# The feed-forward of the last two units of a two-layer attention and MLP kernel, done jointly by Strassen's scheme

## The chip, the cores and the metric

The kernel runs on one core of one Trainium2 chip. A core has five engines with queues of their own: TensorE (PE in the profile; its weight loads are PEld), VectorE (DVE), ScalarE (ACT), GpSimd (POOL) and SyncE (SP), which here only issues transfers. The metric is the device time of one execution in microseconds. The kernel before takes 1161.14 us, the median of three runs (1160.39 to 1161.52).

## The reference

The input x is one sequence of 2048 tokens by 640. Two layers with the same weights run one after the other, each an attention over 8 earlier tokens at distance 2 (32 heads of 20) and then an MLP.

```python
def _A_ref(x, wqkv, wo):
    ...
    logits = jnp.einsum("bhsd,bhswd->bhsw", q, kg) * scale
    logits = jnp.where(mask[None, None, :, :], logits, -1e9)
    attn = _softmax(logits, axis=-1)
    o = jnp.einsum("bhsw,bhswd->bhsd", attn, vg)
    return (lambda x, *d: x.transpose(*d))(o, 0, 2, 1, 3).reshape(B, S, D) @ wo

def _B_ref(x, w1, b1, w2, b2):
    y = _layernorm(x, axis=-1)
    h = _gelu(jnp.einsum("bsd,df->bsf", y, w1) + b1)
    return jnp.einsum("bsf,fd->bsd", h, w2) + b2

x = A_x
x = x + _A_ref(_layernorm(x, axis=-1), A_wqkv, A_wo)
x = x + _B_ref(_layernorm(x, axis=-1), B_w1, B_b1, B_w2, B_b2)
x = x + _A_ref(_layernorm(x, axis=-1), A_wqkv, A_wo)
x = x + _B_ref(_layernorm(x, axis=-1), B_w1, B_b1, B_w2, B_b2)
```

D is 640 and F is 1536.

## The kernel before

The tokens are cut into four groups of 512 (4 row tiles of 128). A group in one layer is a unit; `N` is 8 units, 0 to 7, and units 6 and 7 are the last two groups of the second layer. A unit passes through `layernorm`, `qkv`, `attention` (mostly DVE, in four groups of heads), `project` (the `wo` matmul, L766, and its residual on DVE, L772), a second `layernorm` and `mlp`.

Every matrix product is done in three passes of fp16: both operands are split into a high and a low half, and `PASS` names the pairs (high by high, high by low, low by high). So one step over 128 of K is three matmuls. The weights are scaled by `WS` = 64, split once at the start and kept in DRAM (`mw[0]` for W1, `mw[1]` for W2, twelve blocks of 128 of F each), from where every unit loads them again through the tiles c1 and c2 (names c_78 to c_83 in the order's rows).

`mlp` runs over the twelve F blocks. For each it does 5 K steps of W1 by the transposed activations yT (15 matmuls of 512 columns into a bank ps, L824), the gelu on ACT (L830), the high half on ACT (L833), the low half on DVE (L835), and then for four row tiles the product with W2 (24 matmuls, 512 and 128 columns wide alternately, into five accumulator banks, L846). At the end DVE adds the accumulators to x (L882) and SP stores the rows.

yT comes from DMA transposes that SP issues (L578 after `layernorm`, L755 for the input of `project`). In the last layer the bias b2 is added to x ahead of time, on POOL (L584) or, for unit 7, on DVE (L587).

Nothing runs in the order in which it is written. Each piece of work is given to `Plan` with its engine, a duration, a priority, what it needs and gives, and which buffers it uses; `Plan.run` plays the engines forward with these numbers and writes the instructions out in the order that comes of it. On the chip each engine runs its own queue in that order and waits on semaphores. Operations whose kind stands in `PAIRS` are marked: `Plan` lets long POOL instructions of that kind start only where DVE's marked ones do not run.

## Time and profile before

| what | value |
| --- | --- |
| median of three runs | 1161.14 us |
| span of the profiled execution | 1158.8 us |
| around the span (median less span) | 2.3 us |
| first matmul of all MLPs, L824, share of the chain | 26.6% |
| second matmul, L846, share of the chain | 26.6% |
| qkv, L610, share of the chain | 33.5% |
| `project`, L766, share of the chain | 11.3% |
| last attention instruction on DVE, end | 973.1 us |
| last matmul, end | 1155.17 us |

The profile is one execution recorded by the hardware profiler. The chain of waits starts from the last instruction and goes back, at each step, to what released it; an engine that holds nearly all of the chain sets the time. Rows of groups read: line, engine, operation, tiles out and in, shapes, count, then busy time in us and the mean length of one in ns, then the idle time of the engine before them. Rows of the timeline read: start in us, length in us, engine, line. The end of a matmul is modelled, so lengths of matmul groups are taken from the chain, where one group ends when the next begins.

### The profile page before, as it was taken

The page shows a single profiled execution, that of the slowest core. Times are in us where ns is not written, and L with a number is a line of the kernel's source. Part 1 is how long each engine was busy: PE and PEld are TensorE (multiplying, and loading weights), DVE is VectorE, ACT ScalarE, POOL GpSimd, SP SyncE. Part 2 cuts the span into 40 slices and gives each one's busy share as a digit, 9 for nine tenths or more (in the row PEclk, how much of TensorE's full clock was granted, in tenths as well). Part 3 has the DMA queues.
Part 4 walks back from the last instruction along what each step waited for, and adds up shares of the span by engine and source line. Part 5 has one row for each costly group of instructions (what it writes and reads, how often), then busy time and mean ns, then how long its engine had stood idle before and what let it go on. Part 6 is the DMA issues. An engine that isn't in the chain of part 4 may idle for free.

```text
span 1158.8 us, 17441 instructions
## 1 busy us (share of the span) xinstructions
PE 1153.2 (100%) x6948; PEld 628.1 (54%) x6948; DVE 980.3 (85%) x935; ACT 512.8 (44%) x931; POOL 113.1 (10%) x96
## 2 busy tenths in 40 slices
PE   9999999999999999999999999999999999999998
PEld 6444446577654565546555555555456555555554
DVE  7899999999999999999999999999999995311212
ACT  6395345445464344823537352376235333521211
POOL 1010002011111111210112011101111010000000
PEclk9999999999999999999999999999999999999999
DMA  9999899988686468665746765577555845533432
GB/s 303 311 297 277 292 343 274 280 285 256 190 267 177 165 176 225 194 178 165 231 163 189 194 193 187 175 188 192 189 186 154 265 142 137 140 103 100 147 102 80
DMA packets 219773, 235.01 MB, mean 203 GB/s; under 512 B 129884, under 2 KB 170412, under 8 KB 219692
## 3 DMA queue, kind: packets, MB, share of 16 engines
q1 hardware_dynamic: 219692, 233.90, 67.7%
q8 instruction: 54, 0.88, 0.3%
q14 instruction: 27, 0.22, 0.1%
HBM read 158.93 MB, written 44.78 MB: 176 GB/s over the span
## 4 chain that ended last, share of the span: by engine, by line
PE 98%; DMA 1%; DVE 0%; issue 0%; SPq 0%; ACT 0%; ACTq 0%
PE ps L610 33%; PE acc L846 27%; PE ps L824 27%; PE ps L766 11%; DMA c<-mw 1%; DMA xf<-in_A_x_dram 0%; PE ps L846 0%; DVE wq L433 0%; DVE bn L522 0%; DVE yT L496 0%; DVE w L564 0%; ACT yT L494 0%; DVE xf L882 0%; SPq L445 0%; SPq L428 0%
## 5 line engine op out<-in xcount | busy, mean ns | idle before, releaser
L610 PE MATMUL ps<-wq,yT 128*128 128x480 f16 (+1 forms) x1950 | 391.0, 363 | 0.3
L846 PE MATMUL acc<-c,act 128*128 128x512 f16 (+1 forms) x2298 | 328.6, 299 | 0.3 <-DMA c<-mw 0.3
L824 PE MATMUL ps<-yT,c 128*128 128x512 f16 (+1 forms) x1620 | 328.1, 355 | 0.0
L610 PEld LDWEIGHTS <-yT 128*128 128x128 f16 x1950 | 189.3, 98 | 198.8 <-issue 0.3
L846 PEld LDWEIGHTS <-act 128*128 128x128 f16 x2310 | 181.7, 98 | 142.3 <-issue 0.5
L824 PEld LDWEIGHTS <-c 128*128 128x128 f16 x1620 | 154.6, 98 | 146.3
L830 ACT ACTIVATE act<-ps,b 128x512 f32<-128x512 f32 (+1 forms) x108 | 68.9, 638 | 286.4 <-PE ps L824 285.9
L694 DVE TENSOR_TENSOR pr<-qk 128x2560 f32<-128x2560 f32 x64 | 180.4, 2820 | 3.5 <-DMA qk<-spill 3.5
L720 DVE TENSOR_TENSOR pr<-sm,v 128x2560 f32<-128x2560 f32 x64 | 179.3, 2817 | 0.3
L698 DVE TENSOR_REDUCE sm<-pr 128x128 f32<-128x2560 f32 x64 | 179.5, 2805 | 0.1
L835 DVE TENSOR_TENSOR act<-act 128x512 f16<-128x512 f32 (+1 forms) x108 | 67.5, 626 | 126.2 <-ACT act L833 125.8
L627 ACT ACTIVATE ev<-ps 128x480 f32<-128x480 f32 x128 | 72.6, 569 | 180.3 <-PE ps L610 169.7
L728 DVE TENSOR_TENSOR pr<-pr 128x1280 f32<-128x1280 f32 (+1 forms) x128 | 144.4, 1148 | 0.1
L766 PE MATMUL ps<-wo,yT 128*128 128x320 f16 x960 | 131.7, 299 | 0.0
L766 PEld LDWEIGHTS <-yT 128*128 128x128 f16 x960 | 93.9, 98 | 37.6
L532 ACT ACTIVATE junk<-xf 128x640 f16<-128x640 f32 x57 | 41.9, 734 | 76.2 <-DVE xf L772 63.1
L742 POOL TENSOR_TENSOR ohl<-w,ohl 128x640 f16<-128x640 f32 x24 | 34.3, 1428 | 340.4 <-DVE pr L694 209.7
L549 POOL TENSOR_TENSOR ln<-ln,half 128x2 f32<-128x2 f32 (+1 forms) x31 | 32.8, 1061 | 337.1 <-ACT ln L546 336.9
L833 ACT ACTIVATE act<-act 128x512 f16<-128x512 f32 (+1 forms) x108 | 62.6, 580 | 2.7
L584 POOL TENSOR_TENSOR xf<-xf,b 128x640 f32<-128x640 f32 x26 | 41.1, 1580 | 185.7 <-DVE act L835 67.6
L576 DVE TENSOR_TENSOR w<-w,w 128x640 f16<-128x640 f32 x60 | 47.9, 816 | 6.3 <-ACT w L574 6.3
L568 ACT ACTIVATE w<-xf,ln 128x640 f32<-128x640 f32 x57 | 50.6, 909 | 3.1 <-DVE w L576 3.1
(57 smaller groups left out, 510.2 us busy)
## 6 DMA issues: line engine op xcount, KB each, us to landing
c<-mw SPq DMA_DIRECT2D x216, 320.0 KB, 3.3
spill<-ev SPq DMA_DIRECT2D x64, 480.0 KB, 4.0
qk<-spill SPq DMA_DIRECT2D x32, 880.0 KB, 5.6
v<-spill SPq DMA_DIRECT2D x32, 880.0 KB, 5.3
qk<-spill SPq DMA_DIRECT2D x32, 320.0 KB, 3.5
act<-in_B_w_dram SPq DMA_DIRECT2D x24, 320.0 KB, 5.3
mw<-c SPq DMA_DIRECT2D x24, 320.0 KB, 5.2
xf<-in_A_x_dram SPq DMA_DIRECT2D x16, 320.0 KB, 6.7
```

The costliest lines, as they stand in the source:

```text
L610: nc.tensor.matmul(ps, transposed(yk)[:, a * KD + k, t * P:(t + 1) * P], wq[:, b, k, g, i0:i1], start=first and j == 0, stop=last and j == ...
L627: act(3 * GC, -400 + n, lambda i=i, pk=pk, ek=ek: nc.scalar.activation(tile_of(*ek)[:, :, i], tile_of(*pk)[:, :3 * GC].rearrange("p (a c) ...
L694: nc.vector.tensor_mul(tile_of(*pk), w[:, HALO + m + t0:HALO + m + t0 + EH, None, :].to_broadcast([P, EH, W, GC]), windows(w, t0, [GC, W], ...
L698: dve(E, G - 0.7, lambda pk=pk, t0=t0: nc.vector.tensor_reduce(lg(t0, t0 + EH).rearrange("p t w h -> p (t w h)"), tile_of(*pk).rearrange(" ...
L720: nc.vector.tensor_mul(tile_of(*vk).rearrange("p t w (h d) -> p t (w h) d", d=DH), lg(t0, t0 + EH).rearrange("p t w h -> p t (w h)")[:, :, ...
L728: dve(EH * w * GC, G - 0.9, lambda vk=vk, w=w: nc.vector.tensor_add(tile_of(*vk)[:, :, 0:w], tile_of(*vk)[:, :, 0:w], tile_of(*vk)[:, :, w ...
L766: nc.tensor.matmul(tile_of(*pk)[:, :D // 2], transposed(yk)[:, a * KD + k, t * P:(t + 1) * P], wo[:, b, k, c * D // 2:(c + 1) * D // 2], s ...
L824: nc.tensor.matmul(tile_of(*pk)[:, :nt], tile_of(*ck)[:, a, k * P:(k + 1) * P], transposed(yk)[:, c * KD + k, t0 * P:t1 * P], start=i == 0 ...
L830: act(nt, -430, lambda pk=pk, h32=h32, e=e: nc.scalar.activation(tile_of(*h32)[:, :nt], tile_of(*pk)[:, :nt], AF.Gelu_apprx_tanh, bias=b1[ ...
L833: act(nt, -440, lambda h32=h32, hk=hk: nc.scalar.activation(tile_of(*hk)[:, 0, :nt], tile_of(*h32)[:, :nt], AF.Copy), need=[("h", j)], giv ...
L835: dve(nt, -1000, lambda h32=h32, hk=hk: nc.vector.tensor_sub(tile_of(*hk)[:, 1, :nt], tile_of(*h32)[:, :nt], tile_of(*hk)[:, 0, :nt]), nee ...
L846: nc.tensor.matmul(to, tile_of(*hk)[:, a, (i - t0) * P:(i - t0 + 1) * P], tile_of(*wk)[:, c, w0:w0 + n], start=first, stop=e == NF - 1 and ...
```

## The change

Units 6 and 7 leave `mlp` and are computed together by a new function `pair`. Their 1024 tokens are two blocks of rows (unit 6, unit 7), F is two halves of six blocks, and D is cut into two halves. With blocks A11, A12 (unit 6) and A21, A22 (unit 7), and B11 to B22 of the weights, Winograd's form of Strassen's scheme needs seven products and sums of blocks before and after them.

In the first matmul K is 640, five blocks of 128: the scheme takes blocks 0, 1 and 2, 3 as the two halves of K, and block 4 is added plainly. `joint` makes the operands for this: unit 7's layernorm on ACT, unit 6's once more on DVE, four sums of 256 columns and one of 128 on DVE, a high and a low half of 1536 columns on ACT and DVE, and two transposes per row tile (twelve blocks of 128 each) into zT, which lies over wq. `sums_of_weights` loads the raw weights again, makes four sums for each block pair (W1 on DVE, 256 wide; W2 on POOL, 320 wide), splits them, stores them in `mt` in DRAM and lets the matmuls load them from there.

For each of the six F blocks `pair` first does P1 (A11 by B11), keeps a copy in A21, goes on in the same bank to C11, and does P1 of the second matmul with it. Then, for each block, P6, P5, P7, P4 and P3 in two banks, with DVE adds between (u2, u3, C22, C21, C12), three gelus, the halves, and P2 of the second matmul; then DVE makes S1 and S2 and POOL makes S3 and S4 of the second matmul's rows. At the end the last five products of the second matmul follow each other, 320 columns wide. All matmuls of `second` are 320 wide. Buffers of the attention (wq, wo, v, ev, qk, pr, ohl) and the rows of x of units 0 and 1, once they are stored, hold the new blocks; the lists in `free` say what must be over before.

The bias b2 of both units is added on POOL. The split end of the last unit (`ENDS`, `cuts`, `fresh`) is gone.

```diff
-ENDS = 2
-PARTS = [(0, 0, 2), (0, 2, 4)] + [(b, 0, 4) for b in range(1, 2 * NU)]
+PARTS = [(0, 0, 2), (0, 2, 4)] + [(b, 0, 4) for b in range(1, 2 * NU - 2)]
+PAIR = (2 * NU - 2, 2 * NU - 1)
+KH = 2
+HALF = D // 2
+NP = NF // 2
...
+    T["raw"] = [pr_flat[0][:, :2 * D], pr_flat[0][:, 2 * D:], pr_flat[1][:, :2 * D]]
+    T["thl"] = [pr_flat[1][:, 2 * D:].bitcast(HT), ohl_flat[:, 2 * D:].bitcast(HT)]
...
+    blocks_of = {"A21": cut(v_flat) + [t[:, :BANK] for t in ev_flat], "A11": cut(wo_flat)}
+    for i, q in enumerate(("A12", "S1", "A22", "HL")):
+        blocks_of[q] = spare[i * NP:(i + 1) * NP]
+    last_n, last_u = PAIR[1], PAIR[1] % NU
...
+        "wq": [("qkvp", last_n, t, g) for t in range(M) for g in range(NG)],
+        "pr": [("o", 2 * NU * NG - 1, a) for a in range(M // EH)] + [("done", 0, i) for i in range(M)],
+        "wo": [("wop", last_n, t, c) for t in range(M) for c in range(2)],
+        "ohl": [("oT", last_n, t) for t in range(M)],
+        "blocks": [("hhi", len(PARTS) * NF - 1), ("hlo", len(PARTS) * NF - 1)] + [("done", u, i) for u in range(2) for i in range(M)] + [("zT", t, a) for t in range(M) for a in range(2)],
...
+        for t in range(M):
...
+            act(D, prio, lambda t=t, both=both: ln(both(0, D), u1, t, col), need=[("r", name1, t), *free["wq"], *free["pr"]],
+                give=[("y", name1, t)], use=[lk, zk], ptr=2)
+            dve(D * 3 // 4, prio, lambda t=t, wk=wk: nc.vector.tensor_scalar(
+                tile_of(*wk), x[u0][:, t], col0(2)[:, t:t + 1], col0(3)[:, t:t + 1], op0=OP.mult, op1=OP.add),
+                need=[("r", name0, t), ("r", name1, t)], give=[("again", t)], use=[lk0, wk, zk])
+            for n, u, ready in ((n0, u0, ("again", t)), (n1, u1, ("y", name1, t))):
+                pool(1.6, -100, lambda t=t, u=u: nc.gpsimd.tensor_add(x[u][:, t], x[u][:, t], b2), need=[ready, "b2"], give=[("xb", n, t)])
+            def sums(both=both, wk=wk):
+                Q = KH * P
+                y = tile_of(*wk)
+                a21, a22, s1, s2, s3, s4 = (both(c, c + Q) for c in (0, Q, D, D + Q, D + 2 * Q, D + 3 * Q))
+                nc.vector.tensor_add(s1, a21, a22)
+                nc.vector.tensor_sub(s3, y[:, :Q], a21)
+                nc.vector.tensor_sub(s2, s1, y[:, :Q])
+                nc.vector.tensor_sub(both(D + 4 * Q, D + 4 * Q + P), y[:, 2 * Q:], both(2 * Q, D))
+                nc.vector.tensor_sub(s4, y[:, Q:2 * Q], s2)
...
+            dve(4 * KH * P + P, prio, sums, need=[("y", name1, t), ("again", t)], give=[("zs", t)], use=[zk, wk], more=0.3)
+            act(ZC, prio, lambda zh=zh, both=both: nc.scalar.activation(tile_of(*zh)[:, 0], both(KH * P, KH * P + ZC), AF.Copy),
+                need=[("zs", t)], give=[("zhi", t)], use=[zk, zh])
+            dve(ZC, prio, lambda zh=zh, both=both: nc.vector.tensor_sub(tile_of(*zh)[:, 1], both(KH * P, KH * P + ZC), tile_of(*zh)[:, 0]),
+                need=[("zhi", t)], give=[("zlo", t)], use=[zk, zh])
+            for a in range(2):
+                dma_transpose(prio, lambda t=t, zh=zh, a=a: nc.sync.dma_start_transpose(
+                    zT[:, a * ZK:(a + 1) * ZK, t * P:(t + 1) * P], tile_of(*zh)[:, a]),
+                    need=[("zlo" if a else "zhi", t)], give=[("zT", t, a)], use=[zh])
...
+    def sums_of_weights(i, e, prio):
...
+        def combine():
+            b11, b12, b21, b22 = (part(0), part(n), part(D), part(D + n)) if i else (part(0), part(D), part(n), part(D + n))
+            by = nc.gpsimd if i else nc.vector
+            for to, a, b in ((b11, b12, b11), (b12, b22, b12), (b22, b22, b11), (b21, b21, b22)):
+                by.tensor_sub(to, a, b)
...
+        if i:
+            pool(3.8, prio, combine, need=needs, give=[("tf", i, e)], use=[rk])
+        else:
+            dve(4 * n, prio, combine, need=needs, give=[("tf", i, e)], use=[rk], more=0.3)
+        act(4 * n, prio, lambda: nc.scalar.activation(halves(0), whole(), AF.Copy, scale=WS), need=[("tf", i, e), *free["ohl"]],
+            give=[("thi", i, e)], use=[rk, sk])
+        dve(4 * n, prio, lambda: nc.vector.scalar_tensor_tensor(halves(1), whole(), WS, halves(0), op0=OP.mult, op1=OP.subtract),
+            need=[("thi", i, e)], give=[("tlo", i, e)], use=[rk, sk])
+        dma(P * 16 * n / 1e3, -300 + prio, lambda: nc.sync.dma_start(
+            mt[i][e].rearrange("p a n -> p (a n)"), tile_of(*sk)[:, :8 * n]), need=[("tlo", i, e)], give=[("mt", i, e)], use=[sk], packet=16 * n)
...
+    def pair():
...
+        def second(to, hl, what, e, tiles, passes, start, prio, need, give, use):
...
+            def product():
+                for i in tiles:
+                    for a, c in passes:
+                        nc.tensor.matmul(tile_of(*to(i))[:, :HALF], hl()[:, a, i * P:(i + 1) * P], half_rows(wk, e)[:, c],
+                                         start=start and (a, c) == PASS[0], stop=(a, c) == PASS[-1], skip_group_check=True)
...
+        def split_block(src, dst, tag, prio, need, use=()):
+            act(BANK, prio, lambda: nc.scalar.activation(dst()[:, 0], src(), AF.Copy), need=need, give=[("hi", tag)], use=use)
+            dve(BANK, prio, lambda: nc.vector.tensor_sub(dst()[:, 1], src(), dst()[:, 0]), need=[("hi", tag)], give=[("lo2", tag)], use=use)
...
+        for e in R:
...
+            wt = partial(tile_of, *ck)
+            after = [("wop", n1, M - 1, 1)] if e < 3 else []
+            first(pk, wt, [(k * P, yb(k)) for k in range(KH)], True, j - 1.0 - AHEAD, [*ready, ck, *after] + [("hi", ("P1", e - 2))] * (e > 1),
+                  [("P1", e)], [yk, ck])
+            act(BANK, -435, lambda pk=pk, e=e: nc.scalar.activation(A21[e], tile_of(*pk), AF.Copy), need=[("P1", e), *free["pr"]],
+                give=[("s1", e)], use=[pk])
+            first(pk, wt, [(k * P, yb(k)) for k in range(KH, KD)], False, j - 1.1 - AHEAD, [("s1", e)], [("C11", e)], [yk, ck])
+            gelu(A11[e], partial(tile_of, *pk), e, ("h11", e), [("C11", e), *free["wo"]], [pk])
+            split_block(lambda e=e: A11[e], partial(tile_of, *hk), ("P1", e), -440, [("h11", e)], [hk])
+            for q, passes in enumerate((PASS[:2], PASS[2:])):
+                second(X, partial(tile_of, *hk), "P1", e, range(M), passes, e == 0, j + 0.05 * q,
+                       [("lo2" if q else "hi", ("P1", e)), *([("XP1", e - 1 + q, q ^ 1)] if e + q else [])], [("XP1", e, q)], [hk])
...
+            T = [[(q * KH * P + k * P, zb(z + k)) for k in range(KH)] for q, z in ((0, 3), (3, 5), (2, 7), (1, 0), (4, 9))]
+            B52, B51 = 10 * P, 11 * P
+            pr = j - 1.0 - AHEAD
+            first(bk, wt, T[1], True, pr, [*zready, *got], [("P6", e)], [dk])
+            first(ck, wt, T[0] + [(B52, zb(2))], True, pr + 0.01, [*zready, *got], [("P5", e)], [dk])
+            dve(BANK, -1001, lambda e=e, bk=bk: nc.vector.tensor_add(A12[e], tile_of(*bk), A21[e]), need=[("P6", e), ("s1", e), *free["blocks"]],
+                give=[("u2", e)], use=[bk])
+            first(bk, wt, T[2], False, pr + 0.02, [("u2", e)], [("P7", e)], [dk])
+            dve(BANK, -1001, lambda e=e, bk=bk: nc.vector.tensor_add(A22[e], tile_of(*bk), A21[e]), need=[("P7", e), *free["blocks"]],
+                give=[("u3", e)], use=[bk])
+            dve(BANK, -1000, lambda e=e, ck=ck: nc.vector.tensor_add(A22[e], tile_of(*ck), A22[e]), need=[("P5", e), ("u3", e)],
+                give=[("C22", e)], use=[ck])
+            first(bk, wt, T[3] + [(B51, zb(2))], False, pr + 0.03, [("u3", e)], [("P4", e)], [dk])
+            first(ck, wt, T[4] + [(B52, zb(11))], False, pr + 0.04, [("C22", e)], [("P3", e)], [dk])
+            dve(BANK, -999, lambda e=e, bk=bk: nc.vector.tensor_add(A21[e], tile_of(*bk), A21[e]), need=[("P4", e)],
+                give=[("C21", e)], use=[bk])
+            dve(BANK, -999, lambda e=e, ck=ck: nc.vector.tensor_add(A12[e], tile_of(*ck), A12[e]), need=[("P3", e)],
+                give=[("C12", e)], use=[ck])
+            gelu(A22[e], lambda e=e: A22[e], e + NP, ("h22", e), [("C22", e)])
+            gelu(A21[e], lambda e=e: A21[e], e, ("h21", e), [("C21", e)])
+            gelu(A12[e], lambda e=e: A12[e], e + NP, ("h12", e), [("C12", e)])
+            split_block(lambda e=e: A12[e], partial(tile_of, *hk), ("P2", e), -445, [("h12", e)], [hk])
+            split_block(lambda e=e: A22[e], lambda e=e: hl_of(HL[e]), ("A22", e), 10 + e, [("h22", e)])
+            dve(BANK, 20 + e, lambda e=e: nc.vector.tensor_add(S1[e], A21[e], A22[e]), need=[("h21", e), ("h22", e)], give=[("S1", e)])
+            dve(BANK, 20 + e, lambda e=e: nc.vector.tensor_sub(A22[e], S1[e], A11[e]), need=[("S1", e), ("lo2", ("A22", e))], give=[("S2", e)])
+            pool(1.2, 20 + e, lambda e=e: nc.gpsimd.tensor_sub(A21[e], A11[e], A21[e]), need=[("S1", e)], give=[("S3", e)])
+            pool(1.2, 20 + e, lambda e=e: nc.gpsimd.tensor_sub(A12[e], A12[e], A22[e]), need=[("S2", e), ("lo2", ("P2", e))], give=[("S4", e)])
+            for q, passes in enumerate((PASS[:2], PASS[2:])):
+                second(X, partial(tile_of, *hk), "P2", e, range(M), passes, False, j + 0.05 * q,
+                       [("lo2" if q else "hi", ("P2", e)), *[("s1x", i) for i in range(M)],
+                        *([("XP2", e - 1 + q, q ^ 1)] if e + q else [])], [("XP2", e, q)], [hk])
...
+        plan_of = (("S2", A22, A11, Y, True), ("S1", S1, A22, X2, True), ("S3", A21, S1, Y, False), ("S4", A12, A21, X2, False), ("A22", None, HL, Y, False))
...
```

DVE's queue around the end of the last `project`, before (acc are the accumulators of unit 5, act the halves of h, w the tiles of the layernorm):

```order
L772 SCALAR_TENSOR_TENSOR xf<-ps_94,xf 128x320
L576 TENSOR_TENSOR w_86<-w_88,w_86 128x640
L772 SCALAR_TENSOR_TENSOR xf<-ps_96,xf 128x320
L576 TENSOR_TENSOR w_84<-w_87,w_84 128x640
L576 TENSOR_TENSOR w_87<-w_85,w_87 128x640
L882 SCALAR_TENSOR_TENSOR xf<-acc_101,xf 128x4x128
L835 TENSOR_TENSOR act<-act 128x512
```

The same place now (the first row is the last residual; wq 128x256 and qk_67 are the z tiles, pr the raw weights):

```order
L808 SCALAR_TENSOR_TENSOR xf<-ps_94,xf 128x320
L933 TENSOR_TENSOR qk_67<-qk_67 128x256
L934 TENSOR_TENSOR qk_67<-w_86,qk_67 128x256
L935 TENSOR_TENSOR qk_67<-qk_67,w_86 128x256
L936 TENSOR_TENSOR qk_67<-w_86,qk_67 128x128
L937 TENSOR_TENSOR qk_67<-w_86,qk_67 128x256
L942 TENSOR_TENSOR wq<-wq 128x1536
L973 TENSOR_TENSOR pr_77<-pr_77 128x256 x4
L973 TENSOR_TENSOR pr_76<-pr_76 128x256 x4
L903 SCALAR_TENSOR_TENSOR xf<-acc_99,xf 128x512
L903 SCALAR_TENSOR_TENSOR xf<-acc_100,xf 128x512
L1036 TENSOR_TENSOR act<-wo,act 128x512 x2
```

Sums of the z operands and of the weights now stand between the last residual and the low halves of h (L1036) for which the second matmul waits.

DVE's queue later, in the MLP of unit 7, before:

```order
L882 SCALAR_TENSOR_TENSOR xf<-acc_100,xf 128x512
L835 TENSOR_TENSOR act<-act 128x512
L587 TENSOR_TENSOR xf<-xf,b_105 128x640
L835 TENSOR_TENSOR act<-act 128x512 x2
L587 TENSOR_TENSOR xf<-xf,b_105 128x640
```

DVE's queue now for the fifth block of the six products (L1131 is u2, L1134 u3, L1136 C22, L1140 C21, L1142 C12, L1149 and L1150 S1 and S2, L988 the low halves of W2 sums, L1036 low halves):

```order
L1131 TENSOR_TENSOR xf<-ps_96,ev_70 128x512
L1036 TENSOR_TENSOR act<-xf,act 128x512
L1150 TENSOR_TENSOR wq<-xf,wo 128x512
L988 SCALAR_TENSOR_TENSOR ohl_75<-pr_76,ohl_75 128x1280
L1134 TENSOR_TENSOR qk_67<-ps_96,ev_70 128x512
L1136 TENSOR_TENSOR qk_67<-acc_101,qk_67 128x512
L1036 TENSOR_TENSOR wo<-qk_67,wo 128x512
L988 SCALAR_TENSOR_TENSOR pr_77<-pr_76,pr_77 128x1280
L1140 TENSOR_TENSOR ev_70<-ps_96,ev_70 128x512
L1036 TENSOR_TENSOR act<-qk_67,act 128x512
L1142 TENSOR_TENSOR xf<-acc_101,xf 128x512
```

Where one instruction per block of F stood, ten or eleven now stand, and the adds u2, u3 and C22, which PE waits for before P7, P4 and P3, come in line with the rest.

SP's queue at the start of the stage, before (ohl is the input of `project`):

```order
L817 DMA c_83<-mw_134 128x1280
L755 DMA_TRANSPOSE yT_73<-ohl_75 128x10x128 x4
L817 DMA c_81<-mw_123 128x1280
L817 DMA c_80<-mw_113 128x1280
```

And now:

```order
L840 DMA c_83<-mw_134 128x1280
L960 DMA pr_76<-in_B_w_dram 128x5x128 x4
L791 DMA_TRANSPOSE yT_73<-ohl_75 128x10x128 x4
L1013 DMA c_81<-mw_123 128x2x320
```

Four loads of raw W1 blocks are issued ahead of the transposes of `project`'s input.

And SP's queue now where the loads of the second block of the six products (yT_73) stand; before, this place held loads of c only:

```order
L1121 DMA yT_73<-mt_136 128x2x1024
L1013 DMA c_82<-mw_131 128x2x320
L1013 DMA c_82<-mw_132 128x2x320
L990 DMA mt_139<-pr_77 128x2048
L1013 DMA c_83<-mw_133 128x2x320
L1013 DMA c_83<-mw_134 128x2x320
L1121 DMA yT_73<-mw_118 128x2x384
L1121 DMA yT_73<-mw_112 128x2x128
```

The last two pieces of the second block now follow the store of the fifth block's weight sums (mt_139).

More of the change, by code (lines that the diff above doesn't have):

```diff
@@ L884, in mlp @@
+        for i in tiles:
+            mm(2 * BANK, 2, j, lambda i=i: outer(i, PASS[:2], [own(i)]),
+               need=[("hhi", j), wk, *before], give=[("outh", b, e, i)], use=[wk, hk, bank(i)])
+            mm(BANK, 1, j - 0.1, lambda i=i: outer(i, PASS[2:], [own(i)]),
+               need=[("hlo", j), ("outh", b, e, i)], give=[("out", b, e, i)], use=[wk, hk, bank(i)])
         dve(REST * (t1 - t0), -991, lambda: add(
```

281 lines of the change are left out of this document (220 added, 61 removed).

## The prediction

> **What bounds the kernel now.** I read the page first: busy shares, the slices, the chain of waits.
>
> ```profile
> PE 1153.2 (100%) x6948; PEld 628.1 (54%) x6948; DVE 980.3 (85%) x935; ACT 512.8 (44%) x931; POOL 113.1 (10%) x96
> PE   9999999999999999999999999999999999999998
> DVE  7899999999999999999999999999999995311212
> PEclk9999999999999999999999999999999999999999
> PE 98%; DMA 1%; DVE 0%; issue 0%; SPq 0%; ACT 0%; ACTq 0%
> ```
>
> PE is busy from end to end at full granted clock, and the chain runs through it for 98% of the span. DVE is full for 33 slices and nearly free in the last seven. Busy time alone would not prove a bound, so next come PE's own waits, in total.
>
> ```profile
> PE acc L906 <- POOL ident L404: 1.4, 1, 1.4
> PE acc L846 <- DMA c<-mw: 0.3, 1, 0.3
> ```
>
> In 1158.8 us PE waited twice, for 1.7 us. A matmul less is time less, and any wait added on PE is time more. Then the chain in order of time, for the stretch the change touches (start, length, what).
>
> ```profile
> 973.12 3.26 PE acc L846 x24
> 976.38 3.24 PE ps L824 x15
> 979.62 16.30 PE ps L766 x120
> 995.92 3.26 PE acc L846 x24
> ...
> 1145.36 8.48 PE acc L846 x66
> ...
> 1155.20 0.42 DVE xf L882
> ```
>
> One row of the first matmul (15 of 512 columns, L824) is 3.24 us, or 0.216 us each. One F block of the second (24 matmuls, L846) is 3.26 us. The projection of the last unit shows 120 matmuls of 320 columns in 16.30 us, 0.136 us each: the very shape of the new second matmul. And the busy times of the engines in that stretch:
>
> ```profile
> core 0: us, PE busy (x) PEld busy (x) DVE busy (x) ACT busy (x) POOL busy (x), PEclk, DMA share, GB/s
> 976.22:1155.17 178.95, 178.94 (x1112) 95.40 (x1110) 37.94 (x58) 45.52 (x78) 1.39 (x2) 1.00 0.41 116
> ```
>
> Beside 179 us of PE stand 38 us of DVE, 46 of ACT and 1.4 of POOL. Here is the room that the change spends.
>
> **Matmuls removed.** Before, two units take 24 rows of 3.24 us and 24 of 3.26 us: 156.0 us. After, the first matmul has per block of F, of six, 5 steps of K in the first product and 13 in the other six (54 matmuls), 324 in all: 324 / 15 x 3.24 = 70.0 us. The second has 7 products of 6 blocks, 4 row tiles and 3 passes: 504 matmuls of 320 columns, 504 / 120 x 16.30 = 68.5 us. Together 138.5, so **17.5 us less on PE** (7.8 in the first matmul, 9.8 in the second). K = 640 is why the first gives a tenth and not an eighth: its fifth K block is done plainly. Up to the last blocks of unit 5 the order on every engine is unchanged, so nothing earlier moves.
>
> **What is added, by engine.** Durations by shape:
>
> ```profile
> L728 DVE TENSOR_TENSOR pr<-pr 128x1280 f32<-128x1280 f32 x64 | 94.0, 1482 | 0.0
> L835 DVE TENSOR_TENSOR act<-act 128x512 f16<-128x512 f32 x84 | 57.6, 686 | 126.2 <-ACT act L833 125.8
> L707 DVE TENSOR_TENSOR sm<-sm 128x256 f32<-128x256 f32 x32 | 13.4, 417 | 0.3
> L564 DVE TENSOR_SCALAR w<-xf,bn 128x640 f32<-128x640 f32 x7 | 4.1, 608 | 1.4 <-POOL bn L527 1.4
> 1003.92 0.69 DVE L835 TENSOR_TENSOR act<-act 128x512 f16<-128x512 f32 x1
> 1004.53 2.48 DVE L882 SCALAR_TENSOR_TENSOR xf<-acc,xf 128x512 f32<-128x512 f32 x4
> L584 POOL TENSOR_TENSOR xf<-xf,b 128x640 f32<-128x640 f32 x26 | 41.1, 1580 | 185.7 <-DVE act L835 67.6 <-DVE ohl L742 36.6 <-DVE sm L713 29.0
> ```
>
> Successive DVE instructions start 0.08 us closer than their lengths (0.69 long, 0.61 apart). So, by width and apart: 128 columns 0.2, 256 0.34, 512 0.61, 1280 1.40; on that line 1024 is 1.14 and 1536 is 1.67; a 640-wide scale and shift 0.53. POOL in proportion to 640 columns: 512 takes 1.26, 320 takes 0.79.
>
> *Start of the stage.* PE does the rest of unit 5 first (6.5 us from 976.38, less 1.3 that the order puts later), so the projection starts at 981.6, 2 us later than now, and ends at 997.9. Its input comes by four transposes, with four loads of W1 (320 KB each) now issued ahead of them on SP.
>
> ```profile
> 973.21 6.87 SPq L755 DMA_TRANSPOSE yT<-ohl  x4
> 995.17 3.36 SPq L578 DMA_TRANSPOSE yT<-w  x2
> yT<-w SPq DMA_TRANSPOSE x4, 4.7
> act<-in_B_w_dram SPq DMA_DIRECT2D x24, 320.0 KB, 5.3
> ```
>
> Landing one after the other at 5.3 us bounds the delay at several us, nothing bounds it below; the first transpose has from 973.2 to 981.6 and needs 4.7, so 3.7 are covered. I take 0.4 (0 to 2).
>
> *First product.* It gives PE 90 x 0.216 + 72 x 0.136 + 1.3 = 30.5 us of work, to 1028.4. In it the fourth block's 6 matmuls and 9 matmuls stand back to back in one bank with an ACT copy between. L830 and L833, the nearest rows, bound that copy:
>
> ```profile
> L830 ACT ACTIVATE act<-ps,b 128x512 f32<-128x512 f32 x84 | 57.6, 686 | 255.0 <-PE ps L824 254.8
> L833 ACT ACTIVATE act<-act 128x512 f16<-128x512 f32 x84 | 52.7, 627 | 2.1
> ```
>
> **0.8 us**, with the hand-over on both sides (0.6 to 1.5 if ACT is behind).
>
> *The six z operands.* They must be transposed before the other six products may start. From the last residual (998.6) DVE has in its order three sets of sums (4 x 0.34 + 0.2 = 1.6 each), four low halves of 1536 (6.7), eight weight sums of 256 (2.7), two of 1024 (2.3), two scale-and-shifts (1.1), five of 512 (3.1): 20.6 us, to 1019.2. The last transpose lands 4.7 later, at 1023.9. PE comes at 1029.2. So 5 us of cover: **0** when DVE runs freely. If the cover is gone, each us on DVE is one on PE.
>
> *The six products.* Each block gives PE 39 x 0.216 + 12 x 0.136 = 10.05 us. DVE has per block nine of 512 (5.5), one or two of 1280 and up to three halves of the next stage: 8 to 9 us, so it fits with 1 to 2 us over. In the first block the order lets P4 follow P7 at once, with a DVE add between: **0.9 us** (0.69 and hand-over; 0.7 to 1.5). In later blocks 8 matmuls (1.09 us) stand there, just enough.
>
> *The port.* POOL was idle here; now it gets eight adds of 640 (12.6 us), 24 of 320 (19.0) and 12 of 512 (15.1). How it lives beside DVE (start, length):
>
> ```profile
> 478.90 2.76 DVE L694 TENSOR_TENSOR pr<-qk 128x2560 f32<-128x2560 f32 x1
> 481.58 0.68 DVE L835 TENSOR_TENSOR act<-act 128x512 f16<-128x512 f32 x1
> 480.07 2.13 POOL L549 TENSOR_TENSOR ln<-ln,half 128x2 f32<-128x2 f32 x1 [3.03 <-ACT ln L546]
> 559.44 0.69 POOL L549 TENSOR_TENSOR ln<-ln,half 128x2 f32<-128x2 f32 x1
> 938.70 1.66 POOL L584 TENSOR_TENSOR xf<-xf,b 128x640 f32<-128x640 f32 x1 [6.03 <-DVE act L835]
> 938.86 2.82 DVE L698 TENSOR_REDUCE sm<-pr 128x128 f32<-128x2560 f32 x1
> ```
>
> The same small POOL instruction takes 0.69 us at one place and 2.13 at another, where it sat until DVE's two-operand multiply was over. So one of the two waits. The rows show POOL waiting; the long POOL adds stand where DVE reduces, as at 938.7, so no row shows DVE waiting. Bounds: from 998.6 to the end of the six products DVE has 75 us (20.6; 6.8 of weight sums and halves; 33 for six blocks; 6 of halves done early; 8.4 of 1280) and POOL 47 (two of its 640 adds are over by then, four of 320 come with the first product's end). PE has 90.1. If POOL always waits, nothing is lost. If they exclude one another save for the 30 DVE adds that read a PSUM bank (18 us), the two need 104 us: 14 lost. I take a third, **4.5 us**: DVE's queue is dense, so mostly it holds the port first, as in the row, and POOL's results have time.
>
> By the Trainium skill, SBUF — State Buffer, section Who interferes with whom, a DVE instruction with two SBUF inputs and a GpSimd one that reads SBUF exclude each other, and the second to start blocks for the whole of the first. The trace agrees for POOL's side (2.13 against 0.69); by the rule taken to its end the loss is the 14 us, and the kernel ends near 1160.
>
> *The last five products* have 49 us of PE against 24 halves of 512 on DVE (15 us) and as many on ACT: **0** (up to 2 where the first of them waits for block six). *The end:* the last add is 320 wide, not 256, and the last store 160 KB: **0.2**, between these.
>
> ```profile
> out_dram<-xf SPq DMA_DIRECT2D x1, 192.0 KB, 2.3
> out_dram<-xf SPq DMA_DIRECT2D x1, 128.0 KB, 2.1
> ```
>
> **Sum.** -17.5 + 0.4 + 0.8 + 0.9 + 4.5 + 0.2 = -10.7. The profiled execution spans 1158.8 and the median of the runs is 1161.14, 2.3 more, as work outside the span. So span 1148.1, **time 1150.4 us**.
>
> **Rivals.** *Nothing is lost at the port.* Only the waits that the order forces remain (2.3): 1145.9. For it: POOL is the one that waits in the row, and PE waited only 1.7 us in all under the same planner. Against it: there are no reductions of DVE left to put POOL's new work beside.
>
> *Loads late.* SP issues in order. Each W sum goes DVE, store, load, and blocks of weights stand in SP's queue behind a store that waits for DVE.
>
> ```profile
> mw<-c SPq DMA_DIRECT2D x24, 320.0 KB, 5.2
> c<-mw SPq DMA_DIRECT2D x50, 320.0 KB, 2.9
> ```
>
> Store and load are 8.1 us; the second block's last two pieces stand behind the store of the fifth block's sums, which waits for ACT and DVE at the end of the first product. Its load then lands some 8 us after that, about when PE needs it. A slip of 4 to 8 us there, with half of the port's loss, gives 1152 to 1157, say 1155. Against: transfers fill 0.41 of the engines here.
>
> *DVE becomes the bound* (the other side). If DVE's in-order queue stands still for every POOL instruction, PSUM adds behind it included, 75 + 47 = 122 us meet 90 of PE: 32 lost, 1161.1 - 17.5 + 32 = 1176 at the most. It turns slower than before once some two thirds of POOL's 47 us land on DVE (17.5 less the 2.3 of forced waits is 15.2, and DVE's room is 15: 30 us). I price it at 1168, between that point and the end. For: S3 on POOL starts right at the end of S1, when DVE starts its next two-operand instruction. Against: the 30 PSUM adds have one SBUF operand.
>
> The page TensorE: Matmul & The Clock Gate of the Trainium skill, section What's actually happening, has the clock halved after an idle window of about 3.4 us; a wait that long before the six products would cost another 1.7 us by estimate. No run here shows it: the granted clock is 1.00 and PE never idles so long.
>
> **Chances.** Forecast (1148 to 1153) 0.45; no loss at the port (1145 to 1148) 0.2; late loads (1153 to 1159) 0.2; DVE the bound (above 1159) 0.15, most of it slower. Range 1145 to 1161, which leaves out a tenth above and little below. 0.2% is 2.3 us, about what the measurement can tell from no change: faster is below 1158.8, slower above 1163.5. Faster 0.82, same 0.07, slower 0.11.
>
> **What would show it.** In the changed profile: rows of 15 first-matmul matmuls still at 3.24 us and 120 of the second at 16.3; PE's waits listed at the first product's ACT copy (0.8), at the DVE add after P7 in the first block (0.9), and few others. If the port costs as said, DVE's two-operand instructions of 512 columns show over 0.69 us beside POOL, and PE waits for DVE in the six products by some us. If PE waits for z transposes, the start-stage sum is wrong; if for a load, the second rival; if DVE is at nine tenths from 998 to the end of the six products, the third. A PE sum not 17.5 us smaller would refute the first term itself.

## The result, and the profile after

| what | before | after |
| --- | --- | --- |
| median of the runs | 1161.07 us (6 runs, 1160.39 to 1161.52) | 1165.39 us (6 runs, 1164.25 to 1165.74) |
| span of the profiled execution | 1158.8 us | 1163.8 us |
| PE busy | 1153.2 us | 1142.2 us |
| DVE busy | 980.3 us | 1075.9 us |
| POOL busy | 113.1 us | 192.6 us |

The ratio is 1.0036, 95% interval 1.0025 to 1.0048: the change makes the kernel slower by 4 us, outside the range and on the other side of the forecast.

The page of the changed kernel: busy times, slices, and the engines' shares of the chain.

```profile
PE 1142.2 (98%) x6834; PEld 630.6 (54%) x6834; DVE 1075.9 (92%) x1061; ACT 542.9 (47%) x971; POOL 192.6 (17%) x150
PE   9999999999999999999999999999999999888898
DVE  7999999999999999999999999999999987888871
POOL 1010002011111111210112011101101000368621
PEclk9999999999999999999999999999999999999899
PE 90%; DVE 7%; DMA 1%; ACT 1%; issue 1%; SPq 0%; POOL 0%; DVEq 0%; ACTq 0%; POOLq 0%
```

The last slices carry the result. PE falls below nine tenths exactly where POOL's row rises, and even the granted clock dips. DVE now has 7% of the chain, where it had none. PE's waits, in total:

```profile
PE ps L1063 <- DVE wq L1134: 7.4, 3, 5.5
PE ps L1063 <- ACT v L1084: 3.8, 1, 3.8
PE ps L1063 <- DVE qk L1134: 1.6, 1, 1.6
PE ps L1063 <- ACT ev L1084: 1.4, 1, 1.4
PE acc L1228 <- POOL ident L445: 1.4, 1, 1.4
PE ps L1063 <- DVE xf L1131: 0.9, 1, 0.9
PE ps L847 <- DMA c<-mw: 0.8, 1, 0.8
PE acc L1028 <- ACT act L1035: 0.8, 1, 0.8
```

Without the 1.4 at the start (which the kernel before has too) and the 0.8 ahead of the pair, PE waits 15.9 us in the pair: 9.9 of them for the adds u2 and u3 on DVE (L1131, L1134), 5.2 for the copy of P1 on ACT (L1084), none for a transfer. And after the two longest waits PE is also slow. The timeline of PE (start, length, in brackets the idle time ahead):

```profile
1005.30 5.73 PE L1063 MATMUL ps<-yT,c 128*128 128x512 f16 x18 [3.77 <-ACT v L1084]
1078.94 6.92 PE L1063 MATMUL ps<-wq,yT 128*128 128x512 f16 x18 [5.49 <-DVE wq L1134]
1103.62 4.04 PE L1063 MATMUL ps<-wq,yT 128*128 128x512 f16 x18 [1.55 <-DVE qk L1134]
```

Eighteen such matmuls are 18 x 0.216 = 3.9 us, and a row shows 0.15 more, since the end of its last matmul is modelled. After a wait of 1.55 they take 4.04, so at full speed; after 3.77 they take 5.73, after 5.49 they take 6.92: 1.7 and 2.9 us more. The windows show why: in both stretches the granted clock (PEclk) is below 1 (columns as in the prediction).

```profile
998.00:1010.00 12.00, 8.23 (x33) 3.53 (x32) 11.79 (x21) 6.59 (x11) 5.05 (x4) 0.86 0.73 184
1070.00:1090.00 20.00, 14.51 (x59) 6.38 (x58) 14.77 (x16) 10.05 (x16) 15.26 (x14) 0.83 0.46 150
```

So the account of the span, which grew by 5.0: -17.5 for the matmuls, +15.9 of waits, +4.6 of slow clock, which leaves 2.0. Each of the eight waits comes after a row whose shown end is some 0.15 late, so it is longer by that than listed: 1.2 in all. The 0.8 of a load ahead of the pair, where the kernel before lost 0.3 to a load, is another 0.5. The last 0.3 was not followed.

Both long waits have one form. The first, at the start of the stage: DVE makes the z operands (L933 to L935), POOL adds a bias row (L927), ACT makes high halves (L940) and then the copy of P1 (L1084).

```profile
998.00 1.36 DVE L933 TENSOR_TENSOR wq<-wq 128x256 f32<-128x256 f32 x1
...
1000.96 1.75 DVE L935 TENSOR_TENSOR wq<-wq,w 128x256 f32<-128x256 f32 x1
1003.58 0.41 DVE L933 TENSOR_TENSOR qk<-qk 128x256 f32<-128x256 f32 x1
995.61 6.83 POOL L927 TENSOR_TENSOR xf<-xf,b 128x640 f32<-128x640 f32 x4 [1.40 <-ACT wq L919]
1003.28 1.48 ACT L940 ACTIVATE wq<-wq 128x1536 f16<-128x1536 f32 x1 [5.40 <-DVE wq L937]
1004.67 0.58 ACT L1084 ACTIVATE v<-ps 128x512 f32<-128x512 f32 x1
```

A DVE sum of 256 columns takes 0.41 us when POOL is quiet (1003.58) and 1.36 to 1.75 while POOL adds (995.6 to 1002.4): its length is then about that of one POOL add (6.83 / 4 = 1.7). ACT waits 5.40 us for these sums, and the copy for which PE waits stands behind it in ACT's queue, though it needs nothing of them. PE is idle 3.77.

The second, in the fourth block of the six products:

```profile
1072.35 1.32 DVE L1036 TENSOR_TENSOR act<-xf,act 128x512 f16<-128x512 f32 x1 [2.45 <-ACT act L1035]
1073.60 1.34 DVE L1149 TENSOR_TENSOR xf<-v,wq 128x512 f32<-128x512 f32 x1
1074.86 1.75 DVE L1036 TENSOR_TENSOR wo<-wq,wo 128x512 f16<-128x512 f32 x1
1076.54 1.75 DVE L1150 TENSOR_TENSOR wq<-xf,wo 128x512 f32<-128x512 f32 x1
1078.21 0.68 DVE L1134 TENSOR_TENSOR wq<-ps,ev 128x512 f32<-128x512 f32 x1
1070.39 4.00 POOL L973 TENSOR_TENSOR pr<-pr 128x320 f32<-128x320 f32 x4
1074.35 1.71 POOL L1152 TENSOR_TENSOR xf<-xf,wq 128x512 f32<-128x512 f32 x1
1076.03 1.71 POOL L1151 TENSOR_TENSOR v<-wo,v 128x512 f32<-128x512 f32 x1
```

Four DVE instructions of 512 columns, 0.61 us apart by themselves, take 5.9 us while POOL makes sums of W2 (L973), S4 and S3. The u3 add (L1134) reads a PSUM bank and is not stretched itself (0.68), but it stands behind them, and PE waits 5.49 us for it.

### The profile page after: what moved, and what is told of

It is laid out like the page before. It is cut to its first block, busy times and chain, and to the rows that moved or that the text cites. A ratio compares the mean times of both kernels' runs of the same rounds, so it can differ in the third digit from the quotient of the medians.

```text
span 1163.8 us, 17577 instructions
## 1 busy us (share of the span) xinstructions
PE 1142.2 (98%) x6834; PEld 630.6 (54%) x6834; DVE 1075.9 (92%) x1061; ACT 542.9 (47%) x971; POOL 192.6 (17%) x150
## 4 chain that ended last, share of the span: by engine, by line
PE 90%; DVE 7%; DMA 1%; ACT 1%; issue 1%; SPq 0%; POOL 0%; DVEq 0%; ACTq 0%; POOLq 0%
PE ps L646 33%; PE acc L868 19%; PE ps L847 19%; PE ps L802 11%; PE acc L1028 3%; PE ps L1063 3%; PE ps L1028 2%; PE acc L1228 1%; DMA c<-mw 1%; DVE ohl L988 1%; DVE act L1036 1%; DMA pr<-in_B_w_dram 0%; DVE pr L756 0%; DVE pr L730 0%; DVE pr L764 0%
## 5 line engine op out<-in xcount | busy, mean ns | idle before, releaser
L868 PE MATMUL acc<-c,act 128*128 128x512 f16 (+1 forms) x1728 | 247.9, 299 | 0.0
L847 PE MATMUL ps<-yT,c 128*128 128x512 f16 (+1 forms) x1260 | 246.5, 349 | 0.8 <-DMA c<-mw 0.8
L868 PEld LDWEIGHTS <-act 128*128 128x128 f16 x1728 | 135.9, 98 | 105.8
L847 PEld LDWEIGHTS <-c 128*128 128x128 f16 x1260 | 120.2, 98 | 107.4 <-DMA c<-mw 1.1
L853 ACT ACTIVATE act<-ps,b 128x512 f32<-128x512 f32 (+1 forms) x84 | 52.4, 623 | 170.7 <-PE ps L847 165.2
L623 POOL TENSOR_TENSOR xf<-xf,b 128x640 f32<-128x640 f32 x24 | 37.9, 1578 | 164.8 <-DVE act L858 61.5
L858 DVE TENSOR_TENSOR act<-act 128x512 f16<-128x512 f32 (+1 forms) x84 | 51.1, 609 | 8.8 <-ACT act L856 8.6
L1063 PE MATMUL ps<-wq,yT 128*128 128x512 f16 x180 | 43.8, 398 | 9.9 <-DVE wq L1134 7.4
L608 ACT ACTIVATE w<-xf,ln 128x640 f32<-128x640 f32 x53 | 47.1, 909 | 3.1 <-DVE w L616 3.1
L856 ACT ACTIVATE act<-act 128x512 f16<-128x512 f32 (+1 forms) x84 | 47.5, 566 | 2.0
```

What stands on the lines that cost most here:

```text
L847: nc.tensor.matmul(tile_of(*pk)[:, :nt], tile_of(*ck)[:, a, k * P:(k + 1) * P], transposed(yk)[:, c * KD + k, t0 * P:t1 * P], start=i == 0 ...
L853: act(nt, -430, lambda pk=pk, h32=h32, e=e: nc.scalar.activation(tile_of(*h32)[:, :nt], tile_of(*pk)[:, :nt], AF.Gelu_apprx_tanh, bias=b1[ ...
L868: nc.tensor.matmul(accs[k][:, c0:c0 + n], tile_of(*hk)[:, a, (i - t0) * P:(i - t0 + 1) * P], tile_of(*wk)[:, c, w0:w0 + n], start=first, s ...
L1063: nc.tensor.matmul(ps, wt()[:, a, w0:w0 + P], z(c), start=start and k == 0, stop=k == 3 * len(todo) - 1, skip_group_check=True)
```

## The experiments

The theory is that DVE's instructions with two SBUF operands and POOL's adds exclude one another (the expectations speak of the port, or of the standstill). Its rivals: PE waits for what POOL delivers late; or DVE has too much work in any case. Each ratio is to runs of the kernel before taken alongside, whose medians were 1160.8 to 1161.2 us.

**The collision by itself.** A small kernel with nothing but DVE and POOL in six stages: DVE alone, POOL alone, both, both with a PSUM operand on DVE, both with a one-operand scale and shift on DVE, and both with 320-wide POOL adds.

> This kernel computes nothing of the reference: it runs adds on DVE and POOL alone and together, in six stages. Port theory (a DVE instruction with two SBUF operands and a POOL add exclude each other for their whole length): alone a 512 add on DVE takes 0.69 us and a 640 add on POOL 1.55; together 16 of the one and 6 of the other need the sum of their times, 16 x 0.61 + 6 x 1.5 = 18.8 us, and some DVE instructions show 1.3 us and more; with one operand in a PSUM bank both run side by side, about 10 us, no DVE length over 0.70. Rival (no exclusion, DVE is merely overloaded in the changed kernel): every stage takes the longer of the two alone, about 10 us, with every DVE instruction at 0.69.

Its timeline (L37 DVE two SBUF operands, L40 a PSUM operand, L43 the scale and shift, L46 and L49 POOL):

```profile
17.92 9.08 DVE L37 TENSOR_TENSOR d<-a,b 128x512 f32<-128x512 f32 x12
29.11 9.58 POOL L46 TENSOR_TENSOR g<-a,b 128x640 f32<-128x640 f32 x6
40.12 19.25 DVE L37 TENSOR_TENSOR d<-a,b 128x512 f32<-128x512 f32 x16
40.74 11.54 POOL L46 TENSOR_TENSOR g<-a,b 128x640 f32<-128x640 f32 x6
60.85 11.57 DVE L40 TENSOR_TENSOR d<-bank,a 128x512 f32<-128x512 f32 x16
61.47 9.61 POOL L46 TENSOR_TENSOR g<-a,b 128x640 f32<-128x640 f32 x6
73.90 16.06 DVE L43 TENSOR_SCALAR d<-a 128x640 f32<-128x640 f32 x16
```

Alone, 12 DVE adds take 9.08 (0.757 each, so 16 take 12.1) and six POOL adds 9.58. Together DVE takes 19.25 and POOL 11.54: DVE loses 7.1, POOL 2.0, together 9.1 of POOL's 9.58: they exclude one another nearly for the whole of it. This full DVE queue does not keep POOL out; POOL gets in and DVE pays three quarters of POOL's time. With a PSUM operand neither loses (POOL 9.61, every DVE length 0.69). The 640-wide scale and shift loses too: 16 of them take 16.06, with lengths of 0.49 by the median and up to 1.70. So do DVE's adds beside 320-wide POOL adds (16 in 16.28).

**POOL's new work cut.** Three kernels cut the eight bias adds, the 24 sums of W2, or all of these and S3 and S4 down to one column, with all waits kept; the rest of their results is left out. The third is called "all new POOL work" here, but twelve more adds of 320 columns at the last products (L1101, L1219 and L1223 of the change, 11.5 us) stay on POOL in every version.

```diff
-                pool(1.6, -100, lambda t=t, u=u: nc.gpsimd.tensor_add(x[u][:, t], x[u][:, t], b2), need=[ready, "b2"], give=[("xb", n, t)])
+                pool(1.6, -100, lambda t=t, u=u: nc.gpsimd.tensor_add(x[u][:, t, :1], x[u][:, t, :1], b2[:, :1]), need=[ready, "b2"], give=[("xb", n, t)])
...
-                by.tensor_sub(to, a, b)
+                w = 1 if i else n
+                by.tensor_sub(to[:, :w], a[:, :w], b[:, :w])
```

> The eight bias adds of POOL are cut to one column (b2 is left out of both units but for one column), the order and all else stay. Port theory: the sums of the first z tile take 1.6 us instead of 4.6, the 3.8 us wait of PE for the ACT copy in the first product goes, with the low clock behind it (some 1.8 us): 5 to 6 us faster than the changed kernel, about 1160. If DVE is merely overloaded: within 1 us of 1165.4, since no work of DVE is gone. If loads are late: no change either.

> The 24 sums of W2 on POOL are cut to one column (the sums are wrong beyond it), the order and all else stay. Port theory: in the six products DVE's 1.3 to 1.75 us instructions shrink, ACT no longer waits 2 to 3 us for each sum, the 5.5 us wait of PE at the fourth block goes with the low clock behind it (3.0): 7 to 11 us faster, 1155 to 1158. If DVE is merely overloaded: within 2 us of 1165.4. If loads are late: the 5.5 us stay.

> All of POOL's new work is cut to one column: the bias adds, the W2 sums, S3 and S4 (their results are wrong beyond it); the order, DVE, ACT, PE and the loads stay. Port theory: what is left are the waits that the order forces, 2 to 4 us on PE: 1146 to 1149, all of the 17.5 us less those. If DVE is merely overloaded with its own 75 us: above 1158. If loads are late: PE's waits show DMA as releaser and the time stays above 1155.

| what is cut | median | ratio to before |
| --- | --- | --- |
| nothing (the change) | 1165.39 us | 1.0036 [1.0025, 1.0048] |
| bias adds | 1158.29 us | 0.9975 [0.9965, 0.9984] |
| sums of W2 | 1154.33 us | 0.9949 [0.9932, 0.9966] |
| all new POOL work | 1148.32 us | 0.9891 [0.9876, 0.9906] |

The first two are some 1 to 2 us faster than expected, the third lies inside its 1146 to 1149. From the ratios, bias adds cost 0.61% (7.1 us), sums of W2 0.87% (10.1), all of it 1.45% (16.8); S3 and S4 add nothing that can be told apart. The busy row of the last kernel, and PE's waits in its pair (its lines are one further down: L1135 is u3, L1085 the copy):

```profile
PE 1137.2 (99%) x6834; PEld 630.0 (55%) x6834; DVE 1056.4 (92%) x1061; ACT 542.6 (47%) x971; POOL 137.8 (12%) x150
PEclk9999999999999999999999999999999999999999
...
PE ps L1064 <- DVE xf L1132: 1.8, 1, 1.8
PE ps L1064 <- ACT ev L1085: 1.2, 1, 1.2
PE ps L1064 <- DVE wq L1135: 0.9, 1, 0.9
```

The same 1061 DVE instructions are busy 1056.4 us here and 1075.9 in the change: POOL's work lands on DVE with 19.5 us of standing. Without it PE waits 3.9 us, the clock is full, and the kernel is 12.5 us faster than before. The term of the matmuls is right.

**Results that nobody reads.** The sums of W2 run in full on POOL, but into scratch; the matmuls take unsummed weights. If PE waited for results that come late, this would help; if DVE stands, it would not.

```diff
-                by.tensor_sub(to, a, b)
+                by.tensor_sub(junk.bitcast(FT) if i else to, a, b)
```

> POOL's 24 sums of W2 run at full size but write to a scratch tile that nobody reads, so ACT and DVE no longer wait for their results (the W2 operands stay unsummed). If DVE and ACT were late because they wait for POOL's results: as fast as with the sums cut to one column, 1154. If DVE loses the time because its own two-operand instructions stand still while POOL's run: still 1160 to 1165.

1163.97 us, 1.0021 [1.0011, 1.0030]: by the ratios 1.7 us less than the change, against 10.1 when the sums were cut, and inside the 1160 to 1165 expected if DVE stands. The waits stay nearly as they were (7.4 and 3.8 in the change):

```profile
PE ps L1063 <- DVE wq L1134: 6.2, 3, 4.3
PE ps L1063 <- ACT v L1084: 3.8, 1, 3.8
```

So for the sums of W2 it is not what POOL delivers but that it runs. For the bias adds the trace of the change settles it: no engine is listed there as waiting for L927.

**POOL's work moved to another time.** First the bias adds come behind the six products; then S3 and S4 too; then the sums of W2 go to DVE as well.

```diff
-            for n, u, ready in ((n0, u0, ("again", t)), (n1, u1, ("y", name1, t))):
-                pool(1.6, -100, lambda t=t, u=u: nc.gpsimd.tensor_add(x[u][:, t], x[u][:, t], b2), need=[ready, "b2"], give=[("xb", n, t)])
+            for n, u, ready, pr in ((n0, u0, ("x11", t), 30), (n1, u1, ("XP2", NP - 1, 1), 29)):
+                pool(1.6, pr, lambda t=t, u=u: nc.gpsimd.tensor_add(x[u][:, t], x[u][:, t], b2), need=[ready, "b2"], give=[("xb", n, t)])
...
-            by = nc.gpsimd if i else nc.vector
+            by = nc.vector
```

> The whole computation, with POOL's eight bias adds moved behind the six products. Port theory: the first product and the z operands run as with the bias adds cut, so 1158 to 1160 (1158.3 there), if the adds find room beside the last five products. Rival (they only move the collision): 1163 or more, with PE's waits in the last five products.

> As the run before, and S3 and S4 on POOL moved behind the six products too; the W2 sums stay on POOL among them. Port theory: of POOL's 47 us 19 are left in the six products, where 40 were: 1153 to 1157. Rival (it is the W2 sums alone that matter, by the chain from POOL over ACT to DVE): no gain over the run before, 1158 to 1160.

> As the run before, and the W2 sums done by DVE (24 x 0.4 = 10 us more there), so POOL has nothing long to do until the six products are over. Port theory: DVE's 85 us fit beside 90 us of PE; what is left are the forced waits: 1148 to 1151, a percent faster than before. If DVE is merely overloaded, 10 us more on it make it slower than with the sums on POOL: above 1157.

| version | median | ratio to before |
| --- | --- | --- |
| bias adds late | 1162.34 us | 1.0008 [0.9999, 1.0017] |
| and S3, S4 late | 1164.32 us | 1.0025 [1.0015, 1.0035] |
| and sums of W2 on DVE | 1168.03 us | 1.0061 [1.0049, 1.0074] |

The first gives back at the last products what it gains at the first: the wait of 3.8 for the copy of P1 is gone, and PE waits 3.8 for a residual add (L903) there. That is 2 us above what was expected, and under the rival's 1163. The second is no better, 7 us above its expectation. The third missed its expectation by 17; by its time alone it would fit the rival of too much work on DVE. PE's waits of the third, and its window of the last products:

```profile
PE acc L1028 <- DVE act L1036: 5.2, 1, 5.2
PE ps L1028 <- DVE wo L1036: 4.2, 1, 4.2
...
1100.00:1120.00 20.00, 15.56 (x84) 9.69 (x84) 17.60 (x17) 4.08 (x8) 18.97 (x12) 0.76 0.31 91
```

The six products now run almost freely up to the low half of the sixth block, the wait of 5.2. But POOL is busy for 19 of 20 us at the start of the last five products, where PE needs low halves (L1036, two SBUF operands) from DVE: four of them take 7.57 us from 1105.47, where four would take 2.4 at 0.61 apart. It is the same collision at a new place, with the clock at 0.76. I had counted that stage as free, for DVE has far more time there than work; but PE needs the first halves at once.

**POOL's new work done by DVE.** The same, with bias adds, S3 and S4 on DVE too, so that of the new work POOL keeps the twelve adds of 320 columns at the end; in one version S3 and S4 come late, in the other at their first priority.

```diff
-            pool(1.2, 20 + e, lambda e=e: nc.gpsimd.tensor_sub(A21[e], A11[e], A21[e]), need=[("S1", e)], give=[("S3", e)])
+            dve(BANK, 62 + e, lambda e=e: nc.vector.tensor_sub(A21[e], A11[e], A21[e]), need=[("S1", e)], give=[("S3", e)])
```

> POOL keeps no long two-operand work in the pair: the eight bias adds go to DVE behind the sixth product, the 24 sums for the second matmul's columns and S3 and S4 go to DVE as well, the latter with a lower priority. Standstill theory (what costs the 17 us is that POOL's adds hold the port while DVE's two-SBUF adds stand): 24 x 0.44 + 8 x 0.69 = 16.1 us of new DVE work against about 17.6 us that DVE stood idle from 998 to 1110 us with POOL's work cut; a few of those must lie on the path, so 1148 to 1153 us, PE waits on DVE adds of 0.7 to 2 us apiece and none over 3, granted clock 1.00 throughout. Rival (DVE has too much work in any case, whoever does the rest): 1158 or more, DVE over nine tenths without a break from 998 to 1110 us and PE waits for DVE spread over all products.

> The same, but S3 and S4 keep their first priority, ahead of the sums for P7: DVE spends 8 x 0.69 = 5.5 us more ahead of the first operands that PE needs from them, in return for products that can be interleaved. Standstill theory: 1148 to 1155 us, within 3 us of the run with the low priority. Rival (too much work for DVE): 1158 or more.

All on DVE takes **1152.39 us, 0.9924 [0.9911, 0.9938]**, the only version with the whole computation that is faster than both kernels. It lies inside the expected 1148 to 1153; no wait is over 3 us, as expected, but the clock of 1.00 that was expected with it does not hold in one place. Its busy row, PE's longest group of waits and a window:

```profile
PE 1139.9 (99%) x6834; PEld 630.0 (55%) x6834; DVE 1079.2 (94%) x1105; ACT 543.3 (47%) x971; POOL 126.1 (11%) x106
...
PE ps L1028 <- ACT wo L1035: 3.0, 2, 1.9
...
1100.00:1104.00 4.00, 2.81 (x14) 1.72 (x15) 4.00 (x7) 1.83 (x3) 0.00 (x0) 0.74 0.57 205
```

DVE is busy 1079.2 us, 3.3 more than in the change, although it now does the bias adds, the sums of W2, S3 and S4 as well: doing this work costs DVE 22.8 us (1079.2 - 1056.4; the 16.1 of the expectation left out S3 and S4), letting POOL do it costs 19.5 of standing. POOL took over next to nothing.

With S3 and S4 at their first priority the time is 1161.66 us, 1.0001 [0.9988, 1.0015], 7 us above what was expected; by its time alone it too would fit the rival. PE's longest wait tells why:

```profile
PE ps L1028 <- DMA c<-mt: 9.6, 3, 5.9
```

S3 and S4 stand ahead of the last sums of W2 on DVE. These then reach their store so late that PE waits for the load, which was the prediction's second rival. It is a matter of order: with as much work on DVE, but S3 and S4 late, this wait is gone. So "too much work for DVE" falls.

**The planner told.** POOL keeps its work, and the new kinds are added to `PAIRS`, with the new POOL work marked too.

```diff
-PAIRS = ("qk", "pv", "ad", "o", "sub", "at", "hlo", "yl", "xb", "ol", "wq", "lo", "lm")
+PAIRS = ("qk", "pv", "ad", "o", "sub", "at", "hlo", "yl", "xb", "ol", "wq", "lo", "lm", "again", "zs", "zlo", "tf", "tlo", "lo2", "S1", "S2")
```

> POOL keeps its work, but the planner is told which of the new DVE instructions read two SBUF operands, so that it keeps POOL's adds out of their way where it can. Standstill theory: POOL's 26 us of adds need gaps that a DVE nine tenths busy hardly has, so they come late or take DVE's place as in the plan: 1150 to 1162 us, better than the change, not as good as all on DVE. Rival (too much work for DVE): no better than the change, 1163 or more.

1165.52 us, 1.0034 [1.0021, 1.0048], as slow as the change, so the expected gain is missing. The collision is avoided in the plan (L1134 is down to 0.3), but POOL's sums come late (the last starts at 1119.0, in the change at 1096.5), and PE waits for their load:

```profile
PE ps L1028 <- DMA c<-mt: 10.9, 2, 8.3
PE ps L1063 <- DVE wq L1134: 0.3, 1, 0.3
```

By its time alone this run would fit the rival; its waits are for a load and not for DVE.

## Why the prediction was wrong

**The step that failed** is the port: "I take a third, 4.5 us: DVE's queue is dense, so mostly it holds the port first". Measured, POOL's new work costs 17 us: of the 15.9 us of waits 3.9 are left without it, and the 4.6 of slow clock go. The direction of the mechanism was in the text, both in the bounds (0 to 14) and in the third rival (1168); three things in sizing it were wrong.

1. *Who waits.* The row at 480.07 showed POOL waiting for a long DVE instruction that was already running. It was read as a rule, that DVE comes first in a dense queue. The small kernel shows that this is no rule: beside 16 adds of DVE, POOL lost 2.0 us and DVE 7.1.
2. *The slack.* The bounds set DVE's and POOL's sums (75 and 47 us) against PE's 90 and so gave DVE 15 us of room; the other side was to begin at 30 us of standing. In the run 19.5 us were enough. Slack over a stage covers no wait inside it: PE waits where one add, in order behind four stretched ones, is late by 5.5 us, and gets nothing back where DVE is early. The planner, too, counted these DVE instructions at full speed. That the PSUM adds behind would stand as well was said of the third rival, and priced only in total.
3. *The clock.* The rule of the page TensorE: Matmul & The Clock Gate of the Trainium skill, section What's actually happening, was put aside because PE never idled so long in the profile of before. The change brought idle times of 3.77 and 5.49 us, and 4.6 us of slow clock (1.7 and 2.9, where the prediction's estimate for one such wait was 1.7). The trace agrees with the rule there, at a granted clock of 0.86 and 0.83. That a single long wait is needed is not borne out: the last section has a slow stretch after shorter ones.

By the page SBUF — State Buffer of the Trainium skill, section Who interferes with whom, the one that starts second blocks for the whole of the first. The trace agrees on DVE's side now (1.75 instead of 0.41 us beside a POOL add of 1.7). The prediction's figure by that rule, near 1160, was nearer than mine.

**The other steps.** *Matmuls removed, -17.5:* right; without POOL's new work the kernel is 12.5 us faster, with 3.9 of waits. *P1's copy on ACT, 0.8:* 1.2 without the collision; with it, 1.4 at one block and 3.77 at another, where ACT stood in order behind high halves that wait for DVE (the bound was 1.5 "if ACT is behind"). *P7 and u3 in the first block, 0.9:* 0.9 in the change (one of the three waits for L1134) and in the kernel without POOL's work. A wait for u2 just ahead of it, 0.9 and 1.8, was not foreseen. *z operands, 0:* no wait names a transpose. *Start of the stage, 0.4:* no wait for the transposes of `project`'s input; the projection begins at 982.5, not at 981.6, most of it the 0.8 of the load ahead. *Last five products, 0:* no wait there in the change, but that zero is not safe, as the experiments with late POOL work showed, and the list of POOL's work lacked the twelve adds of 320 columns there. The wait of 0.8 for a high half (L1035) stands at 1019.6, in the first product, and was not foreseen. *Work outside the span, 2.3:* the profiled run of the change took 1165.52 us at a span of 1163.8, so 1.7; the 2.3 set the median of some runs against the span of another.

**The rivals.** *Nothing lost at the port* is refuted by the kernel without POOL's new work. *Loads late* does not happen in the change, where no wait in the pair names a transfer; it lies close, and came up in two experiments. *DVE becomes the bound* had the right mechanism and sign, at 0.15, with 1168 against 1165.4. Its sign in the profile, DVE at nine tenths throughout, shows only at the start:

```profile
998.00:1028.00 30.00, 24.08 (x119) 11.80 (x118) 28.35 (x44) 18.78 (x28) 16.77 (x6) 0.94 0.83 192
1028.00:1096.00 68.00, 59.70 (x287) 28.58 (x286) 56.86 (x62) 32.55 (x48) 48.25 (x38) 0.95 0.73 230
```

28.35 of 30 us, then 56.86 of 68: DVE still has 11 idle us there while PE waits. It is not its throughput that bounds, but its order.

## What to carry to other kernels

Before work is given to an idle engine, ask what it shares with the engine that is to be relieved: here an add on POOL cost DVE, standing, nearly what doing it itself would have cost, and the same arithmetic with all of it on DVE turned 1.0036 into 0.9924. Price a collision at the instructions for which the bound engine waits, with all that stands ahead of them in order, and not as a share of a stage's sum. And after work is moved out of the way of one collision, look at what needs its first operand at once in the place where it went.

## What was not expected of the hardware

- POOL can be kept out as well, for long. One bias add took 11.47 us (maximum of L927), between DVE instructions that follow one another closely, where its neighbours took 1.54 to 1.72:

```profile
L927 POOL TENSOR_TENSOR xf<-xf,b x8: 1542/1720/11474, 995.6 to 1031.0; 128x640 f32<-128x640 f32 x8
```

  So neither engine is simply first; the small kernel's mix does not hold for every sequence. How closely DVE's instructions stand does not decide it alone: in that stretch (1017.9 to 1029.4) each starts some 0.08 us before the one ahead has ended, and so they do at 998 to 1001, where POOL's adds got in each time. What decides was not found.
- A scale and shift with a single SBUF operand (L43 of the small kernel, up to 1.70 us beside POOL, 0.49 by the median) collides with POOL as well, so counting operands does not tell which instructions are safe.
- The clock fell without any wait of 3 us: in the version with all on DVE PE idled 1.1, 0.3 and 1.9 us between 1095.9 and 1101.2, and the granted clock was 0.74 from 1100 to 1104.
